# Shifting one side of the on-chip memory by 32 bytes in a RoPE attention + two FFN kernel on Trainium2

## The chip, the cores and the metric

The kernel runs on one core of a Trainium2 chip (trn2). The metric is device time in microseconds (us) of one execution; lower is better. Three timed executions of the kernel before took 1147.5 to 1148.07 us, median 1147.92 us.

## What is computed

The reference, cut to what matters (4 batches, 8 heads, 576 positions, head size 64, all float32; the two FFNs go 512 -> 2048 -> 512 over 2304 tokens):

```python
q_rot, k_rot = (rotate(q), rotate(k))
scores = scale * np.matmul(q_rot, k_rot.transpose(0, 1, 3, 2))
attn = np.exp(scores - np.max(scores, axis=-1, keepdims=True))
attn = attn / (np.sum(attn, axis=-1, keepdims=True) + 1e-09)
x = np.matmul(attn, v)          # heads side by side: 2304 x 512
h = x @ w_in;   x = (h - np.tanh(h)) @ w_out
h = x @ w_in2;  x = (h * (1.0 / (1.0 + np.exp(-h)))) @ w_out2
```

## The kernel before

**Attention** works on 16 pairs of heads, one after the other. For pair i, `qk_high` (L332, L346) and `qk_low` (L351) transpose the rotated q and k on PE and leave them as a high and a low part: `qs`, `kh`, `kl`. `scores` (L364, L365, L371) multiplies them, 288 columns at a time; `exps`, `transposes` (L466) and `pv` (L498) follow. The tiles of a pair lie in one of two pools: `qk_even` for pairs 0, 2, 4 ..., `qk_odd` for the others.

**The FFNs** are four passes p = 0 to 3: layer p // 2, and half p % 2 of its 16 hidden chunks. A pass goes through five token blocks kb in the order `ORDER[p]`: four of 512 tokens and one, kb = 4, of 256. For each block there are eight *ticks*, one per hidden chunk f. A tick m issues on PE

- `gemm_h(m)` (L685): 12 matmuls into `hp`; the weights `win` are stationary and the token tiles `xh`, `xl` (high and low part of x) are moving, 512 columns (256 for kb = 4);
- `gemm_out(m - 4)` (L761): normally 12 matmuls into `acc`. In layer 1 (p < 2) the weights `wout` are stationary and `gh`, `gl` (high and low part of the activated hidden chunk) are moving. In layer 2 it is the other way round: `gh`, `gl` are stationary and `wout` is moving, always 512 columns.

ACT and DVE turn `hp` into `gh`, `gl` in between (L696 to L730, among them `u`, `s`, `mk`, `t`), and DVE also unpacks the float64 weights for later chunks (`Conv`, L129 to L139). When a block is done, ACT (L767) or DVE (L771, L775) empties `acc`, which has one buffer per chunk, so the next block's `gemm_out` waits for that.

Scheduling is by hand (`tc.manual_schedule`): every engine runs its instructions in program order.

**Where tiles lie.** Pools are opened on the left or the right side of the on-chip memory (SBUF) and are packed from that end. Every partition's right end is at byte 229344, which is 32 more than a multiple of 64; every tile of the right pools has a size that is a multiple of 64 bytes.

```python
qkp[1] = es_odd.enter_context(tc.tile_pool(name="qk_odd", bufs=1, side="left"))
qkp[0] = es_even.enter_context(tc.tile_pool(name="qk_even", bufs=1, side="right"))
rp = es_rope.enter_context(tc.tile_pool(name="rope", bufs=1, side="right"))
pools["sb"] = es_f.enter_context(tc.tile_pool(name="ffn", bufs=1, side="right", reuse_waits="tile"))
pools["x"] = es_o.enter_context(tc.tile_pool(name="ffn_x", bufs=1, side="left", reuse_waits="tile"))
fp = pools["sb" if x % 2 == 0 else "x"]      # L666, where block number x puts its xh and xl
```

- Left, at multiples of 64 bytes: the weights `win`, `wout`, `ident`, everything in pool `attn` (`p`, `pt`, `vm`, `rt`, `sel` ...), `qs`, `kh`, `kl` of odd pairs, and `xh`, `xl` of every second block (x odd: p / kb = 0/1, 0/2, 1/0, 1/4, 2/0, 2/4, 2/3, 3/3, 3/1, 3/4).
- Right, at 32 past a multiple of 64: `qs`, `kh`, `kl` of even pairs, all `rope` tiles, and in the FFNs `xin`, `t`, `u`, `s`, `mk`, all of `gh` and `gl`, and `xh`, `xl` of the other blocks (x even: 0/0, 0/4, 0/3, 1/3, 1/1, 1/2, 2/1, 2/2, 3/0, 3/2; the last block of pass 0 and the first of pass 1 are one block, loaded once).

Of the kernel before, what the change touches and what calls it, by code (L numbers as in the profile page):

```python
# [8 lines left out]
F32 = mybir.dt.float32  # L9
# [20 lines left out]
def kernel(  # L30
# [38 lines left out]

    const = ctx.enter_context(tc.tile_pool(name="const", bufs=1))  # L70
    stage = ctx.enter_context(tc.tile_pool(name="stage", bufs=1))

    ident = const.tile([128, 128], F32, name="ident")
    make_identity(nc, ident)
# [825 lines left out]
```

## Time and profile before

| what | value |
|---|---|
| median of three timed executions | 1147.92 us (1147.5 to 1148.07) |
| span of the profiled execution, first to last instruction | 1145.9 us |
| PE (matmul) busy | 1119.5 us, 98% of the span |
| DVE busy | 785.3 us, 69% |
| ACT busy | 659.2 us, 58% |
| GpSimd (POOL) busy | 268.4 us, 23% |
| attention until the first FFN tick | 0 to 327.8 us |
| FFN ticks | 327.8 us to the end |

The profile shows one execution; its span leaves out what lies before the first and after the last instruction. PE's busy time comes from matmuls that overlap in the pipeline and whose ends are modelled, so it does not say how fast they follow each other; the distance from one matmul's start to the next one's start does. Lines such as L685 are those of the kernel before.

### The profile page before, as it was taken

What the parts mean: (1) busy time and instruction counts of PE and PEld (TensorE: products, weight loads), DVE (VectorE), ACT (ScalarE), POOL (GpSimd) and SP (SyncE); (2) the same over time, 40 slices, a digit from 0 to 9 for tenths busy, and PEclk for the clock granted to TensorE, in tenths of its full rate; (3) what the DMA queues carried; (4) which work ended last, traced back from release to release, by engine and by line L of the source; (5) the groups of instructions that cost most, each with busy time, mean ns of one, the idle gap of its engine ahead of it and who ended that gap; (6) DMA issues with size and microseconds to landing.
All of it is one profiled execution on the core that took longest, in us unless ns stands there. A gap on an engine that the chain in (4) does not pass through costs nothing.

```text
span 1145.9 us, 16928 instructions
## 1 busy us (share of the span) xinstructions
PE 1119.5 (98%) x6032; PEld 902.6 (79%) x6032; DVE 785.3 (69%) x1385; ACT 659.2 (58%) x1431; POOL 268.4 (23%) x359
## 2 busy tenths in 40 slices
PE   5999999999999999999999999999999999999998
PEld 4777777777778889888888898888888888888887
DVE  7778788787858978888899979876544533323323
ACT  4888888788866757766666657534343323222221
POOL 6566676666300101111001001111000000000000
PEclk9999999999999999999999999999999999999999
DMA  4133323232311223221333332432232203122012
GB/s 130 47 99 84 113 68 110 89 94 86 100 64 42 92 74 111 96 89 56 111 129 110 111 120 84 147 111 92 75 110 74 74 1 111 37 74 93 31 44 74
DMA packets 69588, 98.94 MB, mean 86 GB/s; under 512 B 13952, under 2 KB 50432, under 8 KB 67712
## 3 DMA queue, kind: packets, MB, share of 16 engines
q1 hardware_dynamic: 69344, 97.61, 26.3%
q8 instruction: 47, 0.77, 0.3%
q14 instruction: 37, 0.30, 0.1%
q10 hardware_dynamic: 160, 0.26, 0.1%
HBM read 74.25 MB, written 23.59 MB: 85 GB/s over the span
## 4 chain that ended last, share of the span: by engine, by line
PE 91%; DVE 4%; ACT 3%; issue 1%; DMA 0%; SPq 0%; POOL 0%; DVEq 0%; ACTq 0%
PE acc L761 35%; PE hp L685 35%; PE x L498 7%; PE tpp L466 4%; PE sc L364 3%; PE sc L365 2%; PE tpq L332 2%; PE sc L371 1%; ACT p L391 1%; DVE st L377 1%; ACT kh L346 1%; PE sc L446 1%; PE tpb L418 0%; DMA xm<-in_q_dram 0%; DVE wa L136 0%
## 5 line engine op out<-in xcount | busy, mean ns | idle before, releaser
L685 PE MATMUL hp<-xh,win 128*128 128x512 f32 (+1 forms) x1280 | 391.7, 371 | 0.0
L696 ACT ACTIVATE t<-hp 128x512 f32<-128x512 f32 (+1 forms) x160 | 89.0, 557 | 409.7 <-PE hp L685 400.0
L730 DVE TENSOR_TENSOR gl<-t,gh 128x512 fp32r<-128x512 f32 (+1 forms) x160 | 105.9, 662 | 259.5 <-ACT gh L728 259.2
L685 PEld LDWEIGHTS hp<-xh,win 128*128 128x128 f32 x1280 | 233.7, 188 | 46.8 <-issue 1.3
L685 PE MATMUL hp<-xl,win 128*128 128x512 f32 (+1 forms) x640 | 237.0, 370 | 0.0
L761 PE MATMUL acc<-gh,wout 128*128 128x512 f32 (+1 forms) x640 | 196.7, 372 | 1.2 <-ACT u L700 1.2
L761 PE MATMUL acc<-wout,gh 128*128 128x512 f32 x576 | 181.0, 395 | 0.0
L377 DVE TENSOR_REDUCE st<-sc 128x1 f32<-128x576 f32 x144 | 108.7, 755 | 60.0 <-PE sc L446 34.9
L685 PEld LDWEIGHTS hp<-xl,win 128*128 128x128 f32 x640 | 120.2, 188 | 23.2
L761 PEld LDWEIGHTS acc<-gh,wout 128*128 128x128 f32 x640 | 116.7, 188 | 24.9 <-ACT u L700 1.6
L761 PEld LDWEIGHTS acc<-wout,gh 128*128 128x128 f32 x576 | 107.1, 188 | 24.4
L761 PE MATMUL acc<-gl,wout 128*128 128x512 f32 (+1 forms) x320 | 118.9, 372 | 0.0
L153 POOL TENSOR_TENSOR win<-wa,win 128x512 fp32r<-128x512 f32 x32 | 45.4, 1419 | 292.5 <-ACT win L149 292.5
L761 PE MATMUL acc<-wout,gl 128*128 128x512 f32 x288 | 113.8, 395 | 0.0
L391 ACT ACTIVATE p<-sc,st 128x576 f32<-128x576 f32 x144 | 107.0, 743 | 9.4 <-DVE pr L434 7.2
L153 POOL TENSOR_TENSOR wout<-wa,wout 128x512 fp32r<-128x512 f32 x32 | 43.8, 1367 | 284.2 <-ACT wout L149 272.5
L432 ACT ACTIVATE pt<-tpp 128x512 f32<-128x512 f32 x144 | 86.1, 598 | 28.2 <-PE tpp L466 27.4
L728 ACT ACTIVATE gh<-t 128x512 fp32r<-128x512 f32 (+1 forms) x160 | 93.7, 586 | 1.5 <-PE acc L761 1.5
L364 PE MATMUL sc<-kh,qs 128*128 128x288 f32 x256 | 85.4, 348 | 7.1 <-ACT p L391 5.1
L466 PE MATMUL tpp<-ident,p 128*128 128x128 f32 x576 | 87.1, 274 | 0.0
L498 PE MATMUL x<-pt,vm 128*64 128x256 f32 (+1 forms) x512 | 75.8, 418 | 2.1 <-DVE xs L507 1.9
L364 PEld LDWEIGHTS sc<-kh,qs 128*128 128x128 f32 x256 | 49.2, 192 | 34.2 <-ACT p L391 17.8
(112 smaller groups left out, 1798.5 us busy)
## 6 DMA issues: line engine op xcount, KB each, us to landing
raw<-in_moe_w_in_dram SPq DMA_DIRECT2D x32, 512.0 KB, 3.6
raw<-in_moe_w_out_dram SPq DMA_DIRECT2D x32, 512.0 KB, 3.6
xin<-xd SPq DMA_DIRECT2D x14, 1024.0 KB, 4.8
pd<-xo SPq DMA_DIRECT2D x34, 256.0 KB, 2.7
xo<-pd SPq DMA_DIRECT2D x34, 256.0 KB, 4.9
xm<-in_k_dram SPq DMA_DIRECT2D x16, 256.0 KB, 2.9
xm<-in_q_dram SPq DMA_DIRECT2D x16, 256.0 KB, 3.0
vm<-in_v_dram SPq DMA_DIRECT2D x16, 256.0 KB, 2.9
```

Of the source, the lines that this page charges most:

```text
L153: POOL.tensor_tensor(out=w[:, 1], in0=self.val.pop(j), in1=w[:, 0].bitcast(F32), op=ALU.subtract)
L364: PE.matmul(sc[:, e, 0:HALF], lhsT=l, rhs=kh[:, c], start=True, stop=False)
L377: DVE.tensor_reduce(out=st, in_=s_t[g][:, :, 0:HALF], op=ALU.max, axis=AX.XY, negate=True)
L391: ACT.activation(out=p.rearrange("p (e s) -> p e s", e=2), in_=sc[:, :, 0:HALF], func=ACTF.Exp, bias=st, accum_out=sum_t[i][:, n:n + 1])
L432: ACT.activation(out=dst, in_=src, func=ACTF.Copy)
L466: PE.transpose(tp[:, cc * 128:(cc + 1) * 128], p[:, p0 + cc * 128:p0 + (cc + 1) * 128], ident)
L498: PE.matmul(x[o, 0:w], lhsT=l, rhs=r, start=(cc == 0), stop=(cc == NJ))
L685: PE.matmul(hp, lhsT=w[:, a, ws], rhs=bb, start=(n == 0), stop=(n == 3 * KD - 1))
L696: ACT.activation(out=t, in_=hp, func=ACTF.Tanh, scale=0.5 if l else 1.0)
L728: ACT.activation(out=gh, in_=t, func=ACTF.Copy)
L730: DVE.tensor_tensor(out=gl, in0=t, in1=gh.bitcast(F32), op=ALU.subtract)
L761: PE.matmul(acc, lhsT=a, rhs=bb, start=(fi == 0 and n == 0), stop=(fi == NH - 1 and n == 2))
```

## The change

A pool with one tile of 8 float32, 32 bytes per partition, is opened on the right side before any other pool there. Nothing reads or writes that tile.

```diff
     const = ctx.enter_context(tc.tile_pool(name="const", bufs=1))
     stage = ctx.enter_context(tc.tile_pool(name="stage", bufs=1))
+    edge = ctx.enter_context(tc.tile_pool(name="edge", bufs=1, side="right"))
+    edge.tile([128, 8], F32, name="edge")
```

Every tile of a right pool moves down by 32 bytes, from 32 past a multiple of 64 to a multiple of 64 (`xin` from 176096 to 176064, `gh` from 217056 to 217024); no tile on the left moves. The instructions, their order on each engine and their waits stay the same, one for one.

## Rows read from the trace of the kernel before

**Rows 1.** The page, part 1: busy us (share of the span) xinstructions.

```profile
PE 1119.5 (98%) x6032; PEld 902.6 (79%) x6032; DVE 785.3 (69%) x1385; ACT 659.2 (58%) x1431; POOL 268.4 (23%) x359
```

**Rows 2.** The page, part 4: chain that ended last, by line.

```profile
PE acc L761 35%; PE hp L685 35%; PE x L498 7%; PE tpp L466 4%; PE sc L364 3%; PE sc L365 2%; PE tpq L332 2%; PE sc L371 1%; ACT p L391 1%; DVE st L377 1%; ACT kh L346 1%; PE sc L446 1%; PE tpb L418 0%; DMA xm<-in_q_dram 0%; DVE wa L136 0%
```

**Rows 3.** Windows (1/0, 1/1, 1/2, 3/3, 3/0): PE, PEld, DVE, ACT, POOL busy (x), clock, DMA.

```profile
570.20:614.70 44.50, 44.50 (x193) 36.02 (x192) 41.26 (x64) 29.03 (x54) 5.61 (x5) 1.00 0.33 107
614.70:659.50 44.80, 44.80 (x193) 35.98 (x192) 42.51 (x67) 29.25 (x55) 6.36 (x5) 1.00 0.36 118
...
687.90:728.60 40.70, 39.47 (x195) 32.58 (x194) 38.25 (x66) 28.93 (x54) 6.09 (x4) 1.00 0.32 107
...
929.30:973.50 44.20, 44.20 (x194) 36.02 (x193) 12.82 (x20) 13.20 (x24) 0.00 (x0) 1.00 0.21 72
973.50:1018.30 44.80, 44.80 (x194) 36.03 (x193) 15.12 (x24) 11.02 (x20) 0.00 (x0) 1.00 0.20 71
```

**Rows 4.** Timeline of PE, layer 2, block 3/3 (x left): start us, us, instruction.

```profile
940.34 0.39 PE L685 MATMUL hp<-xh,win 128*128 128x512 f32 x1
...
942.83 0.40 PE L685 MATMUL hp<-xh,win 128*128 128x512 f32 x1
943.07 0.62 PE L761 MATMUL acc<-wout,gh 128*128 128x512 f32 x2
...
945.86 0.39 PE L685 MATMUL hp<-xh,win 128*128 128x512 f32 x1
```

**Rows 5.** Timeline of PE, layer 2, block 3/0 (x right).

```profile
979.09 0.39 PE L685 MATMUL hp<-xh,win 128*128 128x512 f32 x1
...
981.89 0.63 PE L761 MATMUL acc<-wout,gh 128*128 128x512 f32 x2
...
984.69 0.39 PE L685 MATMUL hp<-xh,win 128*128 128x512 f32 x1
```

**Rows 6.** Timeline of PE, layer 1, block 1/1 (x right).

```profile
637.12 0.39 PE L685 MATMUL hp<-xh,win 128*128 128x512 f32 x1
...
639.92 0.39 PE L761 MATMUL acc<-gh,wout 128*128 128x512 f32 x1
...
642.72 0.39 PE L685 MATMUL hp<-xh,win 128*128 128x512 f32 x1
```

**Rows 7.** Timeline of PE, layer 1, block 1/0 (x left).

```profile
586.92 0.40 PE L685 MATMUL hp<-xh,win 128*128 128x512 f32 x1
...
587.86 0.39 PE L685 MATMUL hp<-xl,win 128*128 128x512 f32 x1
...
589.45 0.39 PE L685 MATMUL hp<-xh,win 128*128 128x512 f32 x1
589.68 0.40 PE L761 MATMUL acc<-gh,wout 128*128 128x512 f32 x1
```

**Rows 8.** Timeline of PE, a 256-column tick of block 0/4 (x right).

```profile
433.34 0.28 PE L685 MATMUL hp<-xh,win 128*128 128x256 f32 x1
...
436.17 0.28 PE L685 MATMUL hp<-xh,win 128*128 128x256 f32 x1
```

**Rows 9.** Timeline of PE, a 256-column tick of block 1/4 (x left).

```profile
679.35 0.28 PE L685 MATMUL hp<-xh,win 128*128 128x256 f32 x1
...
682.20 0.28 PE L685 MATMUL hp<-xh,win 128*128 128x256 f32 x1
```

**Rows 10.** Windows, sum over the seven even pairs 2, 4 ... 14 of attention.

```profile
sum 138.00, PE 135.29; mean PE 19.33
```

**Rows 11.** Windows, sum over the six odd pairs 3, 5 ... 13.

```profile
sum 118.60, PE 115.67; mean PE 19.28
```

**Rows 12.** Lines L332 and L466: duration ns min/median/max, first and last start us, forms.

```profile
L332 PE MATMUL tpq<-ident,ak x128: 272/273/446, 6.2 to 302.0; 128*128 128x128 f32 x128
...
L466 PE MATMUL tpp<-ident,p x576: 270/272/421, 20.9 to 331.2; 128*128 128x128 f32 x192
```

**Rows 13.** Waits of PE from 349 us on: us in total, times, longest us.

```profile
PE acc L761 <- ACT u L700: 1.2, 1, 1.2
```

## The prediction, made before the changed kernel was run

> **What bounds the kernel now.** I read the page's busy times first. PE is busy for 98% of the span, DVE for 69% [rows 1]. A busy PE can still be a waiting PE, so the chain that ended last comes next: 35% of it is PE on `acc` (L761) and 35% PE on `hp` (L685) [rows 2]. So seven tenths of the time are FFN matmuls that wait for nothing but the matmul before them, and the waits of PE agree: from 349 us to the end there is one, of 1.2 us [rows 13]. Whatever changes the distance between two of these matmuls changes the time; what changes elsewhere is covered.
>
> So the third view is block by block. Each full block holds 192 matmuls of 512 columns, at a granted clock of 1.00, the 2.4 GHz level, and yet blocks differ: 44.80 us for 1/1 and 3/0, 44.50 for 1/0, 44.20 for 3/3 [rows 3]. The blocks of 44.80 have `xh`, `xl` on the right, the others on the left. Nothing else in the program tells 3/0 from 3/3: same shapes, same weights' side, same order. The fourth view, the starts on PE's timeline, says which matmuls it is:
>
> - Both operands on the left (`hp` of block 3/3): twelve distances in 943.07 - 940.34 = 2.73 us, 227.5 ns each; the first eleven of them take 942.83 - 940.34 = 2.49 us, 226.4 each [rows 4]. The twelfth leads to an `acc` matmul, which has an operand on the right.
> - Moving operand on the right (`hp` of 3/0): 981.89 - 979.09 = 2.80 us, 233.3 each [rows 5]. The same in layer 1: 639.92 - 637.12 = 2.80 for `hp`, 642.72 - 639.92 = 2.80 for `acc` with moving `gh`, `gl` [rows 6].
> - Stationary operand on the right, moving one on the left (`acc` in layer 2): 945.86 - 943.07 = 2.79, 232.5 each [rows 4], and 984.69 - 981.89 = 2.80, 233.3 each [rows 5].
>
> One operand on the right, of either kind, costs about 6 ns of 233. All right tiles start 32 bytes past a multiple of 64 and the left ones of these matmuls at a multiple, so "right" and "shifted" cannot be told apart in this trace. I take the shift as the cause: 6 to 7 ns are the time of 16 columns at 2.4 GHz, 6.7 ns, and 16 float32 are 64 bytes, so a read that starts half way into such a piece and so touches one piece more would cost just that. This is a guess that fits, not a measurement.
>
> **What the change does, part by part.** No instruction is added: nothing writes or reads the new tile, and order and waits stay. All that moves is where right tiles start.
>
> *FFN matmuls of 512 columns.* With everything at multiples of 64, each should follow the last after the distance of two aligned operands. I take 227 ns, between the 226.4 and 227.5 above. Counted by the loops:
>
> - `hp`, x on the right: nine block passes of 96, 864 matmuls, 233.3 to 227: 5.4 us.
> - `acc` in layer 1, eight full block passes of 96, 768 matmuls, 233.3 to 227: 4.8 us.
> - `acc` in layer 2: two passes x 8 chunks x 18 groups of 128 tokens x 3 = 864 matmuls, 233 to 227: 5.2 us.
> - `hp` in layer 1, x on the left, three blocks of 96: 230 now, since 589.68 - 586.92 is 2.76 us. There the first four distances take 587.86 - 586.92 = 0.94 us, 235 each, and the next seven 589.45 - 587.86 = 1.59, 227 each [rows 7]: the ticks start slow, behind an `acc` with shifted operands. With aligned ones before them I expect 227: 288 x 3 ns = 0.9 us.
> - `hp` in layer 2, x on the left, 384 matmuls, 227.5 to 227: 0.2 us.
>
> Together 16.5 us. As a check by blocks: 192 x 227 ns is 43.6 us, so a block of 44.80 gives 1.2, one of 44.50 gives 0.9 and one of 44.20 gives 0.6 [rows 3].
>
> The Trainium skill ("TensorE: Matmul & The Clock Gate", section "Back-to-back issue gap") gives the distance of two matmuls by columns and clock alone, N/2.4 + 2.5 ns, without the address; by that the sum would be nothing. The trace disagrees, with 227.5 and 233.3 ns for equal N and clock.
>
> *Matmuls of 256 columns* (576 of them). A tick of 24 takes 436.17 - 433.34 = 2.83 us with x on the right and 682.20 - 679.35 = 2.85 with x on the left [rows 8, 9]. The side does nothing here, so I take zero. Bounds: up to 0.5 us lost, if all ticks come to 2.85; up to 2.6 us gained, if the distance falls from 118 to half of 227, 113.5.
>
> *Attention.* Even pairs have `qs`, `kh`, `kl` on the right, odd ones on the left. Seven even pairs take 138.0 us, 19.71 each, six odd ones 118.6, 19.77 each [rows 10, 11]. Transposes with a shifted stationary operand (L332) last 273 ns at the median, with an aligned one (L466) 272 [rows 12]. So zero, with plus or minus 1 us for 8 even pairs as the bound.
>
> *DVE, ACT and DMA on right tiles.* They keep their durations in this sum; I know of no row that prices them alone, but they are off the chain, and a change of some ns in each would first eat or add slack there.
>
> *What is late next.* A PE that is 3% faster meets the same DVE. In block 1/1 DVE is busy 42.51 of 44.80 us, and 43.6 would still hold it. In block 1/2 it is busy 38.25 of 40.70 us, and the one wait of PE lies there [rows 3, 13]. The wait stands against ACT, but the first `acc` of that block also needs L771 on DVE to have emptied the last one. That block should come down by about 1 us, to 39.7; DVE's work leaves 1.4 us of room in it. So I expect this wait to grow and another to appear before it: 1 us lost, bounds 0 and 3.
>
> Sum: 16.5 - 1.0 = 15.5 us. The span goes from 1145.9 to 1130.4. The median of the timed runs is 1147.92, 2.0 above the span, which I take as unchanged: 1147.9 - 15.5 = **1132.4 us**.
>
> **The rivals.**
>
> 1. *It is the side, not the shift: no change, 1147.9 us.* If right tiles are slow because they lie high in memory, or because the two operands then lie far apart, 32 bytes do nothing. For: the trace has no shifted operand on the left and no aligned one on the right; and the guess of one piece more fails for the short matmuls, as attention with 288 columns shows no difference [rows 10, 11] and 256 columns none either. Against: 6 ns appear for a right operand whether it is the moving or the stationary one, and `xh`, `xl` lie lower than `gh`, `gl` at the same price. The Trainium skill ("SBUF — State Buffer", section "Specifications (TRN2)") gives the memory lines of 16 bytes; by that rule a start at 32 past a multiple of 64 is already at a line's start and the shift changes nothing, so the time would be this rival's. The trace neither shows nor excludes it.
>
> 2. *Only part comes: 1135 to 1143 us.* Either the stationary operand's 6 ns in layer 2 have another cause (`gh`, `gl` are freshly written tiles, weights are not), which takes away 5.2 us: 1137.6. Or only that part comes, which leaves 1147.9 - 5.2 = 1142.7. Or DVE becomes the bound in all of layer 1 and holds its blocks: it is busy 42.51 us in block 1/1, but waits of 0.5 us in each of eight blocks would take 4 us: 1136.4. For: DVE's shares above. Against: the gain per matmul is the same for all three kinds.
>
> 3. *Slower: 1157 us.* The slow start of the ticks in block 1/0 may not come from the shifted `acc` before it but from the aligned operands themselves, two reads that fall on the same piece of memory at the same time. The first four distances there run at 235 ns [rows 7]. If every aligned matmul of 512 columns took 235, against a mean of 232.2 now (864, 768 and 864 at 233, 288 at 230, 384 at 227.5), 3168 x 2.8 ns = 8.9 us would be lost. It decides from a distance of 232.2 ns upward. Against it stands block 3/3, where the first eleven distances run at 226.4 with both operands aligned [rows 4].
>
> **How the numbers follow.** 0.2%, 2.3 us, is about what a measurement of this kernel can tell from no change. My forecast, all of it within some 5 us, gets 0.70; rival 2 gets 0.12, all faster by more than that; rival 1 gets 0.14, no change; rival 3 gets 0.04. So faster 0.82, same 0.14, slower 0.04. The range takes in the forecast with its bounds: downward 226 instead of 227 ns (3.2 us) or the 256-column gain (2.6), not both in full, so 1127.5; upward the DVE wait and rival 2, 1143. Rivals 1 and 3 stay outside, with 0.18.
>
> **What would show it.** In the profile after, a full FFN block should take 43.6 us whichever side x lies on, and every 512-column distance be 226 to 228 ns in both layers. 256-column ticks stay at 2.83 to 2.85 us, pairs of attention at 19.7. PE's waits in layer 1 should grow to about 2 us, before the first `acc` of blocks 1/4 and 1/2. I am wrong if right blocks stay at 44.8 (rival 1), if layer 2's `acc` stays at 233 while `hp` falls (rival 2), or if blocks of 3/3's kind rise (rival 3).

## The result, and the profile after

The changed kernel takes 1131.41 us (median of four runs, 1131.0 to 1131.95), the kernel before 1147.78 beside it (1147.5 to 1148.07): a ratio of 0.986 [0.9847, 0.9874], 16.4 us less. The forecast was 1132.4, within 1127.5 to 1143. The profiled execution has a span of 1129.9 us and took 1131.95. Line numbers from the changed lines on are two higher than before: L687 is `hp`, L763 `acc`.

Busy times and the chain of waits on the page of the changed kernel, the rows that answer to [rows 1, 2]:

```profile
PE 1103.4 (98%) x6032; PEld 903.6 (80%) x6032; DVE 783.9 (69%) x1385; ACT 659.2 (58%) x1431; POOL 269.0 (24%) x359
...
PE acc L763 34%; PE hp L687 34%; PE x L500 7%; PE tpp L468 4%; PE sc L366 3%; PE sc L367 2%; PE tpq L334 2%; PE sc L373 1%; ACT p L393 1%; DVE st L379 1%; ACT kh L348 1%; PE sc L448 1%; PE tpb L420 0%; DVE wa L138 0%; DVE wa L141 0%
```

The same 6032 matmuls, much the same chain, the same 98%: by the shares in these two views nothing has happened. The windows by block show it. Windows of the changed kernel for blocks 1/0, 1/1, 1/2, 3/3 and 3/0, and then for all that follows attention and block 0/0 (columns: stretch, us, busy us and count of PE, PEld, DVE, ACT and POOL, granted clock, DMA share, GB/s):

```profile
565.60:609.10 43.50, 43.50 (x193) 36.03 (x192) 41.20 (x64) 29.03 (x53) 5.68 (x5) 1.00 0.32 109
609.10:652.60 43.50, 43.50 (x193) 36.04 (x192) 41.83 (x67) 29.23 (x55) 6.66 (x5) 1.00 0.37 121
680.90:721.00 40.10, 38.79 (x195) 32.70 (x194) 37.90 (x66) 28.78 (x54) 6.42 (x4) 1.00 0.31 105
917.60:961.10 43.50, 43.50 (x193) 36.05 (x192) 12.81 (x20) 13.14 (x24) 0.00 (x0) 1.00 0.21 73
961.10:1004.60 43.50, 43.50 (x193) 36.04 (x192) 15.11 (x24) 11.02 (x20) 0.00 (x0) 1.00 0.21 73
...
368.30:1129.90 761.60, 755.67 (x3601) 636.42 (x3599) 498.66 (x815) 370.08 (x720) 66.91 (x48) 1.00 0.26 88
```

The last stretch in the kernel before:

```profile
369.20:1145.90 776.70, 770.76 (x3601) 635.25 (x3599) 500.30 (x815) 370.00 (x720) 66.30 (x48) 1.00 0.26 86
```

Blocks of 44.80, 44.50 and 44.20 us [rows 3] have all become 43.50, whichever side x lies on, at the same granted clock of 1.00, the 2.4 GHz level. The stretch from 368.30 on takes 761.60 us where it took 776.70: 15.1 of the span's 16.0 us come from there.

Starts on PE's timeline of the changed kernel, one tick of block 1/1 (layer 1, x right), of 3/3 (layer 2, x left) and of 3/0 (layer 2, x right), which answer to [rows 6, 4, 5], with a tick of the 256-column block 0/4 ahead of them, which answers to [rows 8]. Columns: start us, us, instruction.

```profile
431.40 0.28 PE L687 MATMUL hp<-xh,win 128*128 128x256 f32 x1
...
434.28 0.28 PE L687 MATMUL hp<-xh,win 128*128 128x256 f32 x1
...
614.55 0.39 PE L687 MATMUL hp<-xh,win 128*128 128x512 f32 x1
...
617.27 0.39 PE L763 MATMUL acc<-gh,wout 128*128 128x512 f32 x1
...
619.99 0.39 PE L687 MATMUL hp<-xh,win 128*128 128x512 f32 x1
...
928.49 0.39 PE L687 MATMUL hp<-xh,win 128*128 128x512 f32 x1
...
931.21 0.62 PE L763 MATMUL acc<-wout,gh 128*128 128x512 f32 x2
...
933.93 0.39 PE L687 MATMUL hp<-xh,win 128*128 128x512 f32 x1
...
961.13 0.39 PE L687 MATMUL hp<-xh,win 128*128 128x512 f32 x1
...
963.85 0.61 PE L763 MATMUL acc<-wout,gh 128*128 128x512 f32 x2
...
966.57 0.39 PE L687 MATMUL hp<-xh,win 128*128 128x512 f32 x1
```

Each twelve 512-column matmuls take 2.72 us, 226.7 ns each, for `hp` and `acc`, both layers and both sides. The durations printed beside the starts (0.39) did not move, only the distances did. The 256-column tick went the other way: 434.28 - 431.40 = 2.88 us, 120 ns each, where it was 118.

The single wait of PE from 349 us on ([rows 13] before) and the sum over the seven even pairs of attention ([rows 10] before), both of the changed kernel:

```profile
PE acc L763 <- DVE xo L773: 1.3, 1, 1.3
...
sum 138.00, PE 135.11; mean PE 19.30
```

The wait hardly grew, 1.2 to 1.3 us, and no second one appeared. Attention stands where it stood.

### The profile page after: what moved, and what is told of

Read it like the earlier page. It is cut to its first block, busy times and chain, and to the rows that moved or that the text cites. A ratio compares the mean times of both kernels' runs of the same rounds, so it can differ in the third digit from the quotient of the medians.

```text
span 1129.9 us, 16928 instructions
## 1 busy us (share of the span) xinstructions
PE 1103.4 (98%) x6032; PEld 903.6 (80%) x6032; DVE 783.9 (69%) x1385; ACT 659.2 (58%) x1431; POOL 269.0 (24%) x359
## 4 chain that ended last, share of the span: by engine, by line
PE 90%; DVE 5%; ACT 3%; issue 1%; DMA 0%; SPq 0%; POOL 0%; DVEq 0%; ACTq 0%
PE acc L763 34%; PE hp L687 34%; PE x L500 7%; PE tpp L468 4%; PE sc L366 3%; PE sc L367 2%; PE tpq L334 2%; PE sc L373 1%; ACT p L393 1%; DVE st L379 1%; ACT kh L348 1%; PE sc L448 1%; PE tpb L420 0%; DVE wa L138 0%; DVE wa L141 0%
## 5 line engine op out<-in xcount | busy, mean ns | idle before, releaser
L687 PE MATMUL hp<-xh,win 128*128 128x512 f32 (+1 forms) x1280 | 387.6, 368 | 0.0
L687 PEld LDWEIGHTS hp<-xh,win 128*128 128x128 f32 x1280 | 234.3, 188 | 41.9 <-issue 1.3
L687 PE MATMUL hp<-xl,win 128*128 128x512 f32 (+1 forms) x640 | 235.5, 368 | 0.0
L763 PE MATMUL acc<-gh,wout 128*128 128x512 f32 (+1 forms) x640 | 193.8, 368 | 1.3 <-DVE xo L773 1.3
L763 PE MATMUL acc<-wout,gh 128*128 128x512 f32 x576 | 177.7, 390 | 0.0
L687 PEld LDWEIGHTS hp<-xl,win 128*128 128x128 f32 x640 | 120.7, 189 | 20.5
L763 PEld LDWEIGHTS acc<-gh,wout 128*128 128x128 f32 x640 | 117.2, 189 | 21.8 <-ACT u L702 1.7
L763 PEld LDWEIGHTS acc<-wout,gh 128*128 128x128 f32 x576 | 107.1, 188 | 21.3
L763 PE MATMUL acc<-gl,wout 128*128 128x512 f32 (+1 forms) x320 | 117.8, 368 | 0.0
L763 PE MATMUL acc<-wout,gl 128*128 128x512 f32 x288 | 112.0, 389 | 0.0
```

Source lines behind the costliest of these rows:

```text
L687: PE.matmul(hp, lhsT=w[:, a, ws], rhs=bb, start=(n == 0), stop=(n == 3 * KD - 1))
L763: PE.matmul(acc, lhsT=a, rhs=bb, start=(fi == 0 and n == 0), stop=(fi == NH - 1 and n == 2))
```

## The experiments

Right tiles started 32 bytes past a multiple of 64 before, and start at a multiple now: the theory of the prediction, called A below. But the change did something else too. Worked out from the sizes of the tiles in the code, the weights and the left tiles of the FFN start at 192 modulo 256. The right ones started at 224 and now start at 192: they became *equal* to the left ones modulo 256. Which of the two counts, the trace of the changed kernel cannot tell. Each ratio below is to the kernel before, run beside the experiment.

### Four places that separate "a multiple of 64" from "alike"

The right side moved by 32 bytes more, so that it lies 32 past a multiple of 64 again:

```diff
-    edge.tile([128, 8], F32, name="edge")
+    edge.tile([128, 16], F32, name="edge")
```

> The edge tile is 64 bytes instead of 32: every right tile moves, but starts 32 past a multiple of 64 as before. Theory A (the start of an operand within 64 bytes sets the cost): nothing gained, 1147.8 us, blocks with x on the right 44.8 us. Rival C (any move away from the old addresses helps, the 64 bytes have no part in it): 1131.4 us, blocks of 43.5 us.

Measured: 1146.7 us, ratio 0.9998 [0.9989, 1.0007], no gain. So it isn't any shift that helps. Windows of this kernel, blocks 1/1 and 3/3:

```profile
614.50:659.30 44.80, 44.80 (x194) 36.08 (x193) 42.49 (x67) 29.21 (x55) 6.38 (x5) 1.00 0.36 118
928.90:973.10 44.20, 44.20 (x193) 36.02 (x193) 12.82 (x20) 13.19 (x24) 0.00 (x0) 1.00 0.21 72
```

Then by 64 bytes more than in the change, at multiples of 64 but not equal to the left:

```diff
-    edge.tile([128, 8], F32, name="edge")
+    edge.tile([128, 24], F32, name="edge")
```

> The edge tile is 96 bytes: right tiles start at multiples of 64 again, 64 bytes below those of the change. Theory A: 1131.4 us, all full blocks 43.5 us. If 128 bytes mattered beside 64, it would differ from the change by some ns per matmul, 3168 x 1 ns = 3 us.

Measured: 1143.41 us (1142.71 to 1144.59), ratio 0.9968 [0.9957, 0.998]. A wanted 1131.4 us, so A falls. Windows of this kernel, blocks 1/1, 3/3 and 3/0:

```profile
612.70:657.50 44.80, 44.80 (x194) 35.93 (x193) 42.51 (x67) 29.20 (x55) 6.35 (x5) 1.00 0.36 118
925.80:969.60 43.80, 43.80 (x194) 36.10 (x193) 12.82 (x20) 13.16 (x24) 0.00 (x0) 1.00 0.21 73
969.60:1014.20 44.60, 44.60 (x194) 36.06 (x192) 15.12 (x24) 11.01 (x20) 0.00 (x0) 1.00 0.20 71
```

Block 1/1 is as slow as before the change. The 3.7 us that remain of the gain lie in layer 2's `acc` (229 to 231 ns instead of 233), in the 256-column blocks and in `hp` with x on the left, whose ticks start less slowly (228.3 ns on average in block 1/0, 229.8 before). Starts on PE's timeline of this kernel, block 0/4:

```profile
430.55 0.28 PE L763 MATMUL acc<-gh,wout 128*128 128x256 f32 x1
...
431.91 0.28 PE L687 MATMUL hp<-xh,win 128*128 128x256 f32 x1
...
433.27 0.28 PE L763 MATMUL acc<-gh,wout 128*128 128x256 f32 x1
```

In this tick twelve `acc` and twelve `hp` matmuls take 1.36 us each, 113.3 ns apart, against 118 before and 120 with the change: for 256 columns this place is the better one.

The opposite: the kernel before, with its left tiles moved too, so that *everything* lies 32 past a multiple of 64 and all operands of the FFNs are alike (start equal modulo 256).

```diff
     const = ctx.enter_context(tc.tile_pool(name="const", bufs=1))
     stage = ctx.enter_context(tc.tile_pool(name="stage", bufs=1))
+    const.tile([128, 8], F32, name="pad")
```

> The kernel before, with a 32-byte tile first on the left, so that left tiles too start 32 past a multiple of 64 and both operands of every FFN matmul are shifted alike. Theory A, the two operands' costs not adding: 233.3 ns for all 3168 matmuls of 512 columns instead of 226.7, 1131.4 + 20.9 = 1152 us. Theory A, adding: 240 ns, 1173 us. Rival B (a matmul is slow when its two operands start differently within 64 bytes, and fast when they start alike): 226.7 ns, about 1131 us.

Measured: 1131.19 us, ratio 0.9863 [0.9848, 0.9877]. Not one FFN operand is at a multiple of 64, and the gain is all there. Windows (blocks 1/1, 3/3, 3/0) of this kernel:

```profile
607.80:651.30 43.50, 43.50 (x193) 36.05 (x192) 41.86 (x67) 29.22 (x55) 6.67 (x5) 1.00 0.37 121
916.30:959.90 43.60, 43.60 (x194) 36.11 (x193) 12.81 (x20) 13.14 (x24) 0.00 (x0) 1.00 0.21 73
959.90:1003.40 43.50, 43.50 (x194) 36.04 (x193) 15.11 (x24) 11.02 (x20) 0.00 (x0) 1.00 0.21 73
```

Last, the change with the weights alone moved by 32 bytes, in their own pool; two more pads put the other left tiles back on multiples of 64, 64 bytes from where they were.

```diff
+    wpool[0].tile([128, 8], F32, name="wpad")
...
+        ap.tile([128, 8], F32, name="apad")
...
+        pools["o"].tile([128, 8], F32, name="opad")
```

> The change, with the weight tiles alone moved to 32 past a multiple of 64: stationary in the hp matmuls and in layer 1's acc, moving in layer 2's acc, the other operand aligned. Theory A and rival B: 233.3 ns for all 3168 matmuls, full blocks 44.8 us on both sides, 1152 us. If a stationary operand's shift cost nothing, only layer 2's acc would be slow: 864 x 6.6 ns = 5.7 us, 1137 us.

Measured: 1149.75 us, ratio 1.0026 [1.0016, 1.0035], 0.26% slower than the kernel before and 2 us under the 1152 expected. Now no pair of FFN operands is alike, and block 3/3, 44.20 us before, is as slow as the others. Windows (blocks 1/1, 3/3) of this kernel:

```profile
615.00:659.80 44.80, 44.80 (x194) 36.08 (x193) 42.54 (x67) 29.23 (x55) 6.35 (x5) 1.00 0.35 118
930.00:974.80 44.80, 44.80 (x193) 36.03 (x193) 12.81 (x20) 13.18 (x24) 0.00 (x0) 1.00 0.21 71
```

So what counts is where the two operands of a matmul start *relative to each other*. The next question is in what measure.

### Eight differences in one kernel

The change, with `gh` and `gl` cut out of a wider tile, starting PHASE columns into it: 16, 32, 64, 96 bytes in blocks 0 to 3 of passes 0 and 2, and 128, 160, 192, 224 in passes 1 and 3; zero in block 4.

```diff
+    PHASE = ((4, 8, 16, 24, 0), (32, 40, 48, 56, 0), (4, 8, 16, 24, 0), (32, 40, 48, 56, 0))
+
+    def shifted(m):
+        p, kb, f = SEQ[m]
+        g = pools["sb"].tile([128, 2 * T + 64], F32R, tag="g", name="g", bufs=3)
+        return [g[:, PHASE[p][kb] + i * T:][:, 0:TW[kb]] for i in range(2)]
...
-        gh, gl = tmp(m, "gh", 3, F32R), tmp(m, "gl", 3, F32R)
+        gh, gl = shifted(m)
```

> The change, with gh and gl of one hidden chunk in one tile (4352 bytes) and their start moved within it by 16, 32, 64 and 96 bytes in the blocks 0 to 3 of passes 0 and 2, and by 128, 160, 192 and 224 bytes in the blocks 0 to 3 of passes 1 and 3; nothing else moves, so the other operand of each acc matmul starts 192 past a multiple of 256. Theory A (a start off 64 bytes is slow) expects acc distances of 233 ns at 16, 32, 96, 160 and 224 and 226.7 at 64, 128 and 192; the run with the 96-byte edge already speaks against it. Rival B with 64 bytes expects the same. Theory D (only the difference of the two operands' starts counts, modulo 256 bytes or 128) expects 233 at 32 and 224, some 230 to 233 at 64 and 192, and an open value at the others, 226.7 at 128 if the modulus is 128.

Measured, in a single execution: 1142.72 us. Mean distance of 512-column `acc` matmuls by the difference, from the starts on PE's timeline (`g` moves in layer 1, is stationary in layer 2; at 192 bytes the first value has a wait of PE in it):

```
bytes        0      16     32     64     96     128    160    192    224
moving ns    226.7  231.4  233.6  230.3  234.6  232.6  233.4  234.1  233.5
station. ns  226.7  226.7  232.7  233.2  234.1  233.0  233.2  229.3  232.7
```

The rows for 128 bytes, blocks 1/0 (`g` moving) and 3/0 (`g` stationary), on PE's timeline of this kernel:

```profile
599.63 2.95 PE L770 MATMUL acc<-g,wout 128*128 128x512 f32 x12
...
602.42 0.39 PE L687 MATMUL hp<-xh,win 128*128 128x512 f32 x1
...
994.49 2.96 PE L770 MATMUL acc<-wout,g 128*128 128x512 f32 x12
...
997.29 0.40 PE L687 MATMUL hp<-xh,win 128*128 128x512 f32 x1
```

Twelve distances are 2.79 and 2.80 us, 232.5 and 233.3 ns each. A measure of 64 or of 128 bytes would have made 64 or 128 as good as zero; neither is. Between 32 and 224 nearly everything costs 6 to 8 ns.

The table also holds a direction. In its second row it is the other operand that is moved, so counted as the moving operand's start minus the stationary one's, modulo 256, that row runs backwards: its 64 is 192. Counted so, the two rows agree within 1.5 ns at every difference that both have: 230.3 and 229.3 ns at 64, 234.1 and 233.2 at 192. Layer 2's `acc` in the second experiment, at 64, has 230.2. So a moving operand that starts 64 bytes above the stationary one costs some 3 ns and one 64 below it 7; 16 above costs 4.7, and 16 below (the second row's 16) nothing.

### How the cost depends on the width

The kernel before, with each `hp` of 512 columns cut in two, 480 and 32, 448 and 64, 384 and 128, 320 and 192 in passes 0 to 3:

```diff
+        cut = (480, 448, 384, 320)[p] if TW[kb] == T else TW[kb]
+        for c0, c1 in ((0, cut), (cut, TW[kb])):
...
-                PE.matmul(hp, lhsT=w[:, a, ws], rhs=bb, start=(n == 0), stop=(n == 3 * KD - 1))
+                    PE.matmul(hp[:, c0:c1], lhsT=w[:, a, ws], rhs=bb, start=(n == 0), stop=(n == 3 * KD - 1))
```

> The kernel before, each hp group of 12 matmuls of 512 columns issued as two groups: the first 480, 448, 384 or 320 columns in passes 0 to 3, then the rest; blocks with x on the left have both operands alike, those on the right differ by 32 bytes. If the 6 ns of a shifted operand are one more piece of 64 bytes, they appear at each width. If they grow with the columns, the distance of shifted operands is 1.097 cycles a column (438.7, 409.6, 351, 292.5 ns x 0.4167... that is 219.4, 204.7, 175.5, 146.3 ns at 480, 448, 384, 320), and of equal ones 32 cycles more than the columns, as at 256 and 512 in the trace of the change: 213.3, 200, 173.3, 146.7 ns. The kernel takes longer as a whole, some 1200 us.

(In that text 219.4, 204.7, 175.5 and 146.3 ns are the expected distances of unlike operands; the four larger numbers before them are a slip.) Measured, in a single execution: 1247.67 us, longer for the added matmuls. Mean distance within a tick, median over the ticks, x right (32 bytes off) against x left (alike): 219.9 against 216.6 ns at 480 columns, 206.5 against 202.5 at 448, 176.8 against 176.0 at 384, 146.5 against 146.5 at 320. Starts on PE's timeline of this kernel, 448 columns, blocks 1/0 (x left) and 1/1 (x right):

```profile
641.37 0.36 PE L689 MATMUL hp<-xh,win 128*128 128x448 f32 x1
...
642.98 0.57 PE L689 MATMUL hp<-xh,win 128*128 128x448 f32 x2
...
687.49 0.37 PE L689 MATMUL hp<-xh,win 128*128 128x448 f32 x1
...
689.14 0.58 PE L689 MATMUL hp<-xh,win 128*128 128x448 f32 x2
```

Eight distances: 1.61 us against 1.65. What unlike operands cost is no constant piece more: over 6 ns at 512 columns, 3 to 4 at 480 and 448, nothing at 320, and at 256 it turns into a gain. The prediction's picture, one extra 64-byte piece per matmul, falls with this as well.

### Is the measure 256 bytes?

If the difference counts modulo 256 (theory D), then moving the right side by 256 bytes more than the change must keep all the gain, and by 128 more must lose it.

```diff
-    edge.tile([128, 8], F32, name="edge")
+    edge.tile([128, 72], F32, name="edge")
```

> The edge tile is 288 bytes, 256 more than in the change. Theory D (only the difference of the two operands' starts modulo 256 bytes counts, and zero is fast): as the change, 1131.4 us, full blocks 43.5 us. If the modulus were larger than 256 this run would be slow, some 1143 to 1148 us.

Measured: 1131.56 us, ratio 0.9862 [0.9848, 0.9877].

```diff
-    edge.tile([128, 8], F32, name="edge")
+    edge.tile([128, 40], F32, name="edge")
```

> The edge tile is 160 bytes, 128 more than in the change: right tiles start at multiples of 64, and 128 away from the left ones modulo 256. Theory A (multiples of 64) and a modulus of 128: 1131.4 us. Theory D with 256: slow, right blocks 44.7 us, acc at 232.6 to 233 ns as with 128 bytes in the run of phases, 1146 us.

Measured: 1146.73 us, ratio 0.9999 [0.9989, 1.0008], though every tile is at a multiple of 64, even of 128 relative to the left. Window of block 1/1 in the kernel with 256 bytes more:

```profile
608.00:651.50 43.50, 43.50 (x194) 36.03 (x193) 41.86 (x67) 29.24 (x55) 6.62 (x5) 1.00 0.36 121
```

and in the kernel with 128 bytes more:

```profile
612.90:657.70 44.80, 44.80 (x194) 36.04 (x193) 42.51 (x67) 29.24 (x55) 6.38 (x5) 1.00 0.36 118
```

D holds in both.

### A place for the 256-column matmuls too

The change by itself, run again as the base of this group:

> The change once more, on the chip of the next three runs: 0.986 of the kernel before, 1131.4 us.

Measured: 1131.38 us (1130.72 to 1131.66), ratio 0.9862 [0.9848, 0.9875].

To it, a start 192 bytes into their tiles for the moving operands of the 256-column matmuls (x in block 4 of both layers, `g` in layer 1), since those ran fastest unlike:

```diff
+    NARROW = 48
...
+        hi, lo = (z[:, NARROW:NARROW + w] if w < T else z for z in (hi, lo))
...
-        return pools["sb"].tile([128, T], dt, tag=tag, name=tag, bufs=bufs)[:, 0:TW[SEQ[m][1]]]
+        w = TW[SEQ[m][1]]
+        at = NARROW if w < T and SEQ[m][0] < 2 and tag in ("gh", "gl") else 0
+        return pools["sb"].tile([128, T], dt, tag=tag, name=tag, bufs=bufs)[:, at:at + w]
```

> The change, with the moving tiles of the 256-column matmuls (xh, xl of block 4 in both layers, gh and gl of block 4 in layer 1) started 192 bytes into their tiles. In the run with the 96-byte edge, where these differ from the weights by 64 bytes the other way, 256 columns took 113.7 ns instead of 120. Theory D: 576 matmuls (384 hp, 192 acc) x 6 ns = 3.5 us less than the change, 1128 us. If the time of a 256-column matmul passes on to the ones behind it, less, down to nothing.

Measured: 1129.35 us (1128.9 to 1129.8), ratio 0.9845 [0.9831, 0.9858]: 2.0 us under the change beside it, with ranges that don't meet. It beats both kernels. Windows (blocks 0/4 and 1/4) of this kernel:

```profile
410.80:438.60 27.80, 27.80 (x193) 25.93 (x192) 19.48 (x45) 18.13 (x48) 0.00 (x0) 1.00 0.26 92
651.00:678.90 27.90, 27.90 (x194) 26.02 (x193) 21.87 (x49) 16.38 (x45) 0.00 (x0) 1.00 0.38 128
```

and of the changed kernel:

```profile
411.80:440.10 28.30, 28.30 (x194) 26.33 (x193) 19.61 (x45) 18.33 (x49) 0.00 (x0) 1.00 0.26 93
652.60:680.90 28.30, 28.30 (x194) 26.30 (x193) 21.92 (x49) 16.42 (x45) 0.00 (x0) 1.00 0.38 130
```

Half a microsecond less in each. The distance is 117.8 ns, not the 113.3 of the second experiment. The rest of the 2.0 us lies in blocks 2/4 and 3/4 and in the 512-column matmuls that follow 256-column ones: in the changed kernel five of the eight `hp` ticks in block 0/2 come behind 256-column `acc` matmuls, and their first five distances are 229 to 236 ns (mean of the block 228.1); here they are 226.7.

The same start for `kh` and `kl` in attention, on top of the change:

```diff
-            qk_t[i] = [qkp[i % 2].tile([128, 2 * S + (REM if nm != "qs" else 0)], F32R, tag=nm, name=nm, bufs=1)
+            qk_t[i] = [qkp[i % 2].tile([128, 2 * S + (REM + 64 if nm != "qs" else 0)], F32R, tag=nm, name=nm, bufs=1)
...
+            qk_t[i][1:] = [z[:, 48:48 + 2 * S + REM] for z in qk_t[i][1:]]
```

> The change, with kh and kl started 192 bytes into wider tiles, so that in the scores they differ from qs by 192 bytes in the first half and by 64 in the second (128 more), instead of 0 and 128. If 288 columns gain as 256 do, 640 matmuls x up to 6 ns = up to 4 us less, of which the part counts in which PE waits for nothing; between 1127 and 1131.4 us. If attention is held by the chain over ACT and DVE, no change.

Measured: 1131.17 us (1130.19 to 1132.26), ratio 0.9861 [0.9847, 0.9874], no difference to the change: the score matmuls' mean distance, waits included, went from 160.6 to 159.4 ns (160.1 in the run of both edits below), and the time didn't follow. And both edits together:

> Both edits of the two runs before: the sum of their gains, 1124 to 1128 us.

Measured: 1129.33 us (1128.87 to 1130.24), ratio 0.9846 [0.9833, 0.986], as with the 256-column edit alone.

## Why the prediction came out right in its time and wrong in its reason

- **Counts and prices held.** 3168 matmuls were to go to 227 ns and went to 226.7 in most ticks (227.2 on average), in every kind that the prediction listed; blocks were to come to 43.6 us and came to 43.50. Reading the distances by block and side was enough for that, since the change made the slow blocks into the fast kind, whatever sets the two kinds apart.
- **The step that failed: "I take the shift as the cause".** The start of one operand within 64 bytes doesn't matter: with all operands off a multiple of 64 the whole gain is there (1131.19 us), with all on one it can be gone (1146.73). What the runs show in its place: at 512 columns a matmul has the short distance when both its operands start alike modulo 256 bytes. The kernel before could not tell side, shift and difference apart, as the prediction said of the first two; the third it did not see. That this shift to a multiple of 64 also made the starts equal modulo 256 was luck: of the two other shifts to a multiple of 64, for which the prediction's reason gives the same gain, one gave 1143.41 us and the other 1146.73. The extra 64-byte piece, too, fitted 6.7 ns by coincidence.
- **Why attention did not move.** The prediction took zero from equal pairs. The addresses give the reason: `qs`, `kh` and `kl` of one pair start alike, on either side, before as after, and the score matmuls of either side differ by 0 or 128 bytes. A shift by 32 of all three changes no difference. At its 288 columns attention speaks against A; the prediction listed it under rival 1 and gave that too little weight.
- **Rival 1** (no change) rested on the side, and fell. The Trainium skill ("SBUF — State Buffer", section "Specifications (TRN2)") gives lines of 16 bytes. That a start 32 past a multiple of 64 costs nothing by itself agrees with the 1131.19 us; but that the time stays, which rival 1 drew from it, does not follow, because the length of a line says nothing of where two operands lie relative to each other.
- **Rival 3's picture**, two reads that collide when they fall alike, is the wrong way round at 512 columns. At 256 columns its sign is right: alike operands take 120 ns, unlike ones 113 to 119.
- **Sizes that were off.** Summed over the starts of both traces, the 512-column distances take 16.6 us less, where the prediction had 16.5. With 226.7 ns everywhere it would have been 17.5, but matmuls in the first block and behind 256-column ones stay slower. The term of 1.0 us for PE's wait was about 0.1: block 1/2 came down to 40.10 us, not to 39.7, DVE was busy 37.90 of it, and the room was enough. The 256-column matmuls, taken as zero, lose 0.8 us (from 118.2 to 119.6 ns, mean of 576), outside the stated bound of 0.5 on that side. 16.6 - 0.1 - 0.8 = 15.7 us in the FFNs, and with 0.3 outside them 16.0 in the span, where 15.5 was forecast. The other half of the 1.0 us by which the forecast is too high lies in what the timed runs add to the span, 1131.41 - 1129.9 = 1.5 us instead of 2.0. So errors of opposite signs, in the wait and the 256-column matmuls, nearly cancelled.

**Still open** is what happens inside. A matmul reads its moving operand while the weights of a matmul behind it are being loaded, and PEld's 36 us of 43.5 in each block leave little time without such a load; two reads that walk through memory in step and never meet would explain why alike is good. That was argued, not tested. One place in the traces bears on it. The last `hp` of a layer 2 tick with x on the left is alike with its own weights, but the weights loaded next, `gh` for `acc`, start 32 bytes off. In the kernel before, all 28 such distances are 235 ns, where the five ahead of them average 226.7 ([rows 4] has one, 943.07 - 942.83); with the change they are 227. So the cost appears before the first unlike matmul has started. Whether a matmul's own weights cost anything was not separated, because alike matmuls behind unlike ones start slow as well. Nor is it settled why the direction counts, why the sign turns between 320 and 256 columns, why 192 bytes gave 113.3 ns in one kernel and 117.8 in another, or whether the measure of 256 holds for other types or widths.

## What to carry to other kernels

Where long runs of 512-column float32r matmuls bound a kernel, try starting their moving and stationary tiles at the same address modulo 256 bytes: here that was 2.8% per matmul (233.3 to 226.7 ns) and 1.4% of the kernel, for a tile that nobody reads. Look for such a cost in the start-to-start distances on PE's timeline, grouped by where the operands lie; busy shares, durations and the chain did not show it. And when rows of one trace differ in several things at once, list all of them, the operands' relation to each other included, and run the one placement that separates them before naming a cause.

## What the runs showed of the hardware that was not expected

- The distance of back-to-back matmuls depends on the difference of the two operands' start addresses modulo 256 bytes: 226.7 ns at 0 and mostly 232 to 235 ns at 32 to 224 bytes, for 512 columns at the 2.4 GHz level; 128 more loses all of the gain, 256 more none. The direction counts: 229 to 230 ns where the moving operand starts 64 bytes above the stationary one, 233 to 234 where it starts 64 below.
- The sign depends on the width: alike wins 4 ns at 448 columns, nothing at 320, and loses at 256 (120 ns against 113 to 119). In cycles at 2.4 GHz, 226.7 and 120 ns are 544 and 288: the columns and 32 more. At 480 and 448 columns alike matmuls stood some 3 ns above that.
- The cost is passed on: behind 256-column matmuls at 120 ns the first five distances of a 512-column tick are 229 to 236 ns, and with ones at 117.8 before them 226.7.
- The Trainium skill ("TensorE: Matmul & The Clock Gate", section "Back-to-back issue gap") gives the isolated distance as N/2.4 + 2.5 ns, which makes an estimate of 215.8 at 512 columns, and some 131 for a stream of weight loads and matmuls. The traces agree with neither: no tick of 512-column float32r matmuls read here had a mean distance under 226; why they stand some 11 ns above the formula was not tried.
